# Fused attention and two feed-forward layers: score tiles kept in two standing PSUM buffers, written bank 1, 2, 0, and k/q transposes ahead of the fp32 ones

## The chip, the cores and the metric

The kernel runs on one core of a Trainium2 chip. A core has a matrix engine (TensorE, "PE" in the profile; its weight loads are "PEld"), a vector engine (DVE), a scalar engine (ACT), a general engine (GpSimd, "POOL"), a sync engine (SP) that issues DMAs, and 16 DMA engines. Each engine works through its own queue in the order of the program; engines wait for each other through semaphores. Matmul results go to PSUM, which is divided into banks of 512 fp32 columns. The metric is the device time of one execution in microseconds (us). Lower is better.

## The reference

```python
# q, k, v: (2, 8, 1152, 64) fp32
q_pool = q.reshape(B, H, S // 2, 2, D).mean(axis=3)          # 576 rows per head
scores = scale * np.matmul(q_pool, k.transpose(0, 1, 3, 2))  # 576 x 1152
scores = scores - np.max(scores, axis=-1, keepdims=True)
attn = np.exp(scores)
attn = attn / (np.sum(attn, axis=-1, keepdims=True) + 1e-09)
x = np.matmul(attn, v)                                       # then (1152, 512)
# then RMS norm, silu(x @ w_gate) * (x @ w_val) @ w_out,
# then h = x @ w_in;  out = (h * tanh(softplus(h))) @ w_out2
```

## The kernel before

fp32 operands are split into two fp16 halves, "hi" and "lo", and each product is made from three fp16 products (hi hi, hi lo, lo hi). The attention takes the first 275 us or so of the span, the two feed-forward layers the rest.

**Turns.** Attention is worked through two heads at a time. A pair of heads (`g` = 0 to 7, called pairs 1 to 8 below) has nine turns (`j` = 0 to 8), so there are 72 turns (`n` = 9 g + j). A turn is one block of 128 pooled query rows against all 1152 keys of a head; the turn for j = 8 holds the last 64 rows of each of the two heads. `attn_step(n)` (L700 to L722) writes a turn's instructions, and since the kernel runs under a manual schedule, the order of these calls is the order of each engine's queue:

- `scores(n)` (L237): PE writes a tile `s` of three PSUM banks, 384 columns used in each. Per bank there are two matmuls that add up in it (four of half width for j = 8). `ps_s` is a pool of two such tiles, taken in turn.
- `flip_pe(n-1)` (L297): three fp32 transposes on PE of a part of the turn before's exponentials `e`, into `ep`.
- `each(n, "pe")` calls `kq_flip` (L187): at j = 4 to 8, PE transposes up to eight fp16 blocks of the next pair's k and q (`khl`, `qhl`), into bank 0 of the tile `s` of turn n-1, whose scores have by then been read by the exponential.
- `split_hi`, `split_lo` and `flip` (n-1): ACT rounds a part of `e` to fp16 (`hl`, L282), POOL makes the lo half (L134), and SP issues a DMA transpose into `et`.
- `part_hi(n-1)` (L307): ACT rounds `ep` into `et` (L309).
- `each(n, "act")`: ACT casts of the next pair's k, q and v (L154, L178).
- `row_max(n)` (L259): DVE takes the maximum of the 1152 scores (L262) and scales it (L263).
- `each(n, "dve")` calls `kq_keep` (L201): at j = 4 to 8, DVE copies the transposed k and q out of bank 0 into `kqT` of the next pair (L203). This is the eviction of the title.
- `part_lo(n-1)` (L311): DVE makes the lo half of `ep` (L134 on DVE, `et<-ep,et`).
- `row_exp(n)` (L266): ACT's exponential of the whole tile `s` (L269).
- `attn_v(n-5)` (L319): 27 matmuls on PE (54 for j = 8) that weight v by `et` of five turns before, into `av`; then DVE's division (L356, L368, L370) where a block of x is done.
- `each(n, "scale")`: a DVE scaling of k, q or v (L141, L172) in some turns.

The tile `s` of turn n-1 is used again by `scores(n+1)`. The pool hands it over as a whole, so the first matmul of `scores(n+1)` stands behind the eviction that DVE makes in turn n. On DVE that eviction stands behind `row_max(n)`.

From n = 46 on, DVE, ACT and POOL also do RMS-norm steps (L461 to L490), and from n = 57 on the first steps of the weights' unpacking (`job_step`; L393 to L411), in between.

Of the kernel before, what the change touches and what calls it, by code (L numbers as in the profile page):

```python
# [9 lines left out]
F32 = mybir.dt.float32  # L10
F16 = mybir.dt.float16
# [29 lines left out]
def kernel(  # L41
# [13 lines left out]
    nc = tc.nc  # L55
# [16 lines left out]
    NTI = 2 * NI + 1  # L72
    NPR = B * NP
    NIT = B * NP * NTI
    SC = 3
# [5 lines left out]
    def pool(name, bufs, side="left", **kw):  # L81
        return tc.alloc_tile_pool(name=name, bufs=bufs, side=side, reuse_waits="tile", **kw)
# [28 lines left out]
    nat, kqT, vvt, cvt = {}, {}, {}, {}  # L111

    def load(w, g, i, eng=nc.scalar):

        if g >= NPR:
            return
        b, h0 = g // NP, 2 * (g % NP)
        if i == 0:
            nat[w, g] = nat_p.tile([128, 2, NJ, D] if w != "q" else [128, NTI, 2, D], F32, tag="nat", name=w + "n")
        t = nat[w, g]  # L120
        nm = NI * 128 * 2
        if w != "q":
            eng.dma_start(out=t[:, i], in_=(k if w == "k" else v)[b, h0 + i].rearrange("(p j) d -> p j d", j=NJ))
        elif i < 2:
            eng.dma_start(
                out=t[:, i * NI:(i + 1) * NI], in_=q[b, h0 + i, 0:nm, :].rearrange("(p i r) d -> p i r d", i=NI, r=2))
        else:
            for e in range(2):
                eng.dma_start(out=t[e * TL:(e + 1) * TL, 2 * NI],
                                  in_=q[b, h0 + e, nm:, :].rearrange("(p r) d -> p r d", r=2))  # L130
# [7 lines left out]
    def kv_scale(w, g):  # L138

        t = nat[w, g].rearrange("p h j (d z) -> p z (h j d)", z=2)  # L140
        nc.vector.tensor_scalar(out=t, in0=t, scalar1=QK_S if w == "k" else V_S, scalar2=None, op0=ALU.mult)  # L141

    def kv_hi(w, g, e):
        if e == 0:
            if w == "k":
                cvt["k", g] = cv_p.tile([128, 2 * NJ, 2 * D], F16, tag="khl", name="khl")
            else:
                t = kq_p.tile([128, 2 * NJ, 2 * D + 2], F16, tag="vv", name="vv")
                nc.gpsimd.memset(t[:, :, 2 * D:2 * D + 1], 1.0)
                vvt[g] = t  # L150
        t = (cvt["k", g] if w == "k" else vvt[g])[:, e * NJ:(e + 1) * NJ, :]
        o = 0 if w == "k" else D
        sc = 1.0 if g else QK_S if w == "k" else V_S
        nc.scalar.activation(out=t[:, :, o:o + D], in_=nat[w, g][:, e], func=ACTF.Copy, scale=sc)  # L154

    def kv_lo(w, g, e):
        t = (cvt["k", g] if w == "k" else vvt[g])[:, e * NJ:(e + 1) * NJ, :]
        o = 0 if w == "k" else D
        sc = 1.0 if g else QK_S if w == "k" else V_S
        lo_op(nc.gpsimd if g else nc.vector, t[:, :, D - o:2 * D - o], nat[w, g][:, e], sc, t[:, :, o:o + D])  # L160
        if e == 1:
            del nat[w, g]
# [11 lines left out]
    def q_hi(g):  # L174

        t = cv_p.tile([128, NTI, 3, D], F16, tag="qhl", name="qhl")
        a = cvt["s", g]
        nc.scalar.activation(out=t[:, :, 0:3:2, :], in_=a.unsqueeze(2).to_broadcast([128, NTI, 2, D]), func=ACTF.Copy)  # L178
        cvt["q", g] = t
# [18 lines left out]
            nc.tensor.transpose(out=ps[:, s - s0, :], in_=src, identity=ident)  # L198
        flips[g, s0] = (ps, n)

    def kq_keep(g, s0):  # L201
        ps, n = flips.pop((g, s0))
        nc.vector.tensor_copy(out=kqT[g][:, s0:s0 + n, :], in_=ps[:, 0:n, :])  # L203

    def kq_first():

        t = kqT[0] = kq_p.tile([128, 2 * NJ + 2 * NTI, 128], F16, tag="kqT", name="kqT")
        for s0, n in ((2 * NJ, 2 * NTI), (0, 2 * NJ)):
            e = 0 if s0 else 1
            kv_hi("v", 0, e)  # L210
            kv_lo("v", 0, e)
            ps = ps_s.tile([128, SC, 512], F32, tag="s", name="s").bitcast(F16)
            for s in range(s0, s0 + n):
                w, z = divmod(s - 2 * NJ, NTI)
                if s < 2 * NJ:
                    src = cvt["k", 0][:, s, :]
                else:
                    src = cvt["q", 0][:, z, w:w + 2, :].rearrange("p t d -> p (t d)")
                c, o = divmod(s - s0, 8)
                nc.tensor.transpose(out=ps[:, c, o * 128:(o + 1) * 128], in_=src, identity=ident)  # L220
            for c in range(-(-n // 8)):
                z = min(8, n - 8 * c)
                o = t[:, s0 + 8 * c:s0 + 8 * c + z, :]
                i = ps[:, c, 0:z * 128].rearrange("p (s t) -> p s t", s=z)
                if c == 1:
                    nc.vector.tensor_copy(out=o, in_=i)
                else:
                    nc.scalar.activation(out=o, in_=i, func=ACTF.Copy)

    def where(n):  # L230

        g, j = divmod(n, NTI)
        return g // NP, g, (j if g < NPR - 1 else (j - 1) % NTI)

    s_t, e_t, hl_t, et_t, av_t = {}, {}, {}, {}, {}

    def scores(n):  # L237
        b, g, j = where(n)
        kt = kqT[g][:, 0:2 * NJ, :]
        qt = kqT[g][:, 2 * NJ:, :]  # L240
        ps = ps_s.tile([128, SC, 512], F32, tag="s", name="s")
        heads = [(j % 2, j % 2 * NI + j // 2, 0, 128)] if j < 2 * NI else [
            (e, 2 * NI, e * TL, TL) for e in range(2)]
        per = SN // 128
        for c in range(SC):
            for e, slot, p0, m in heads:
                for w in range(2):
                    nc.tensor.matmul(  # L248
                        out=ps[p0:p0 + m, c, 0:SN],
                        lhsT=qt[:, w * NTI + slot, p0:p0 + m],  # L250
                        rhs=kt[:, e * NJ + c * per:e * NJ + (c + 1) * per, :].rearrange("p j t -> p (j t)"),
                        start=(w == 0),
                        stop=(w == 1),
                    )
        s_t[n] = ps

    mx, read = {}, {}
# [39 lines left out]
    def flip_pe(n):  # L297

        if n < 0:
            return  # L300
        e = e_t[n]
        ps = ps_t.tile([128, PB, 128], F32, tag="t", name="ep")
        for s in range(PB):
            nc.tensor.transpose(out=ps[:, s, :], in_=e[:, (NB + s) * 128:(NB + s + 1) * 128], identity=idf)  # L304
        ep_t[n] = ps
# [352 lines left out]
    def each(n, engine):  # L658

        g, j = n // NTI + 1, n % NTI  # L660
        if g >= NPR:
            return
        if engine == "load":
            if j in (0, 2):
                load("v", g, j // 2)
            elif j in (3, 4):
                load("k", g + 1, j - 3)
            elif j >= 6:
                load("q", g + 1, j - 6)
        elif engine == "act":  # L670
            if j in (2, 3):
                kv_hi("k", g, j - 2)
            elif j == 4:
                q_hi(g)
            elif j in (7, 8):
                kv_hi("v", g, j - 7)
        elif engine == "scale":
            if j in (1, 6):
                kv_scale("v" if j == 6 else "k", g)
            elif j == 2:  # L680
                q_scale(g)
        elif engine == "pool":
            if j in (2, 3):
                kv_lo("k", g, j - 2)
            elif j == 1:
                q_add(g)
            elif j == 4:
                q_lo(g)
            elif j in (7, 8):
                kv_lo("v", g, j - 7)  # L690
        elif j in FJ:
            f = FL[FJ.index(j)]
            if engine == "pe":
                kq_flip(read[n - 1], g, *f)
            else:
                kq_keep(g, f[0])

    FJ = (4, 5, 6, 7, 8)

    def attn_step(n):  # L700
        scores(n)
        flip_pe(n - 1)
        each(n, "pe")
        split_hi(n - 1)
        if n:
            split_lo(n - 1)
            flip(n - 1)
        part_hi(n - 1)
        x_sums()
        each(n, "act")  # L710
        row_max(n)
        each(n, "dve")
        part_lo(n - 1)
        row_exp(n)
        each(n, "pool")
        each(n, "load")
        if n >= LAG:
            attn_v(n - LAG)
            attn_r(n - LAG)
            attn_x(n - LAG)  # L720
        each(n, "scale")
        read.pop(n - 1, None)  # L722

    with tc.manual_schedule():
        nc.scalar.preload_act_table_set("natural_log_exp_and_others")
        ps_av = pool("ps_av", 1, space=PSUM)
        ps_t = pool("ps_t", 1, space=PSUM)
        ps_s = pool("ps_s", 2, space=PSUM)

        for w, i in (("q", 0), ("q", 1), ("q", 2), ("k", 0), ("k", 1), ("v", 0), ("v", 1)):  # L730
            load(w, 0, i, nc.sync)
# [61 lines left out]
        for step in TAIL:  # L793
# [5 lines left out]
            else:  # L799
                n = NIT - LAG + int(step)  # L800
# [114 lines left out]
```

## Time and profile before

| | us |
|---|---|
| median of 3 runs | 692.02 (690.71 to 693.10) |
| the profiled execution | 695.35 |
| its span, first to last instruction | 693.6 |
| attention, from the span's start | about 275 |

In the span's 693.6 us, PE is busy for 608.0 us, DVE for 462.5, ACT for 390.4 and POOL for 323.2. The span has two parts with different limits, and the page's row of slices shows them: in the slices of the attention DVE is at 8 and 9 tenths and PE at 7 or so, and after the attention PE is at 9 tenths. A row of a timeline gives the start (us from the span's start), the duration, the engine, the line, what is written and read, and in square brackets the time for which the engine had been idle and what ended that. Rows of matmuls are merged (x6 is six of them), and their ends are modelled.

### The profile page before, as it was taken

To read this page: it belongs to the slowest core of one execution; us is meant where nothing else is said; L and a number is where in the kernel's file an instruction comes from. 1 tells how busy PE (TensorE), PEld (TensorE's weight loads), DVE (VectorE), ACT (ScalarE), POOL (GpSimd) and SP (SyncE) were. 2 spreads that over 40 slices of the span, in tenths; PEclk is the share of its full clock that TensorE was granted. 3 is DMA by queue.
4 is the path that set the end of the run, shared out by engine and by line. 5 is a ranking of instruction groups with operands and counts; after the bars stand their busy time and mean duration, and the time that the engine had idled before them with its cause. 6 is when DMAs were issued, how large, how long until landed. Compare 5 with 4: busy or idle time off the path is not lost.

```text
span 693.6 us, 14705 instructions
## 1 busy us (share of the span) xinstructions
PE 608.0 (88%) x5880; PEld 428.1 (62%) x5880; DVE 462.5 (67%) x750; ACT 390.4 (56%) x654; POOL 323.2 (47%) x250
## 2 busy tenths in 40 slices
PE   3787778787676667799999999998999999999997
PEld 2466565666555556677777677776755555555553
DVE  4788888888899987559999962189289921111110
ACT  4888888898688586555555543144176623222221
POOL 0867878687689563057787772144033310000000
PEclk9799999999999899999999999999999999999999
DMA  6799899899899895344554430255245201000101
GB/s 185 135 191 185 175 179 171 185 186 176 150 172 222 171 186 104 71 122 124 156 175 156 153 122 1 61 167 168 62 126 176 95 0 46 1 1 15 31 1 45
DMA packets 161908, 84.05 MB, mean 121 GB/s; under 512 B 124720, under 2 KB 152368, under 8 KB 161840
## 3 DMA queue, kind: packets, MB, share of 16 engines
q1 hardware_dynamic: 151184, 67.71, 44.7%
q10 hardware_dynamic: 10656, 15.40, 8.4%
q8 instruction: 46, 0.75, 0.5%
q14 instruction: 22, 0.18, 0.1%
HBM read 50.07 MB, written 2.36 MB: 76 GB/s over the span
## 4 chain that ended last, share of the span: by engine, by line
PE 52%; DVE 32%; issue 7%; ACT 6%; DMA 2%; POOL 1%; SPq 0%; ACTq 0%; DVEq 0%
DVE m L262 9%; DVE c L402 6%; PE z L511 5%; PE z L513 4%; PE z L512 4%; PE po L648 4%; PE po L647 4%; PE po L646 4%; PE s L248 4%; ACT e L269 3%; PE py L511 3%; PE py L513 3%; PE py L512 3%; DVE c L400 3%; DVE c L404 2%
## 5 line engine op out<-in xcount | busy, mean ns | idle before, releaser
L134 POOL TENSOR_TENSOR hl<-e,hl 128x768 f16<-128x768 f32 x71 | 117.5, 1655 | 79.8 <-ACT hl L282 44.2
L248 PE MATMUL s<-kqT 128*128 128x384 f16 (+1 forms) x480 | 87.9, 342 | 28.3 <-DVE kqT L203 26.3
L269 ACT ACTIVATE e<-s,m 128x1152 f32<-128x1152 f32 x72 | 87.7, 1218 | 39.4 <-DVE m L263 35.2
L262 DVE TENSOR_REDUCE m<-s 128x1 f32<-128x1152 f32 x72 | 97.3, 1351 | 16.3 <-PE s L248 15.7
L136 DVE SCALAR_TENSOR_TENSOR g<-mo,g 128x384 f16<-128x384 f32 x48 | 26.9, 561 | 100.6 <-ACT g L621 100.6
L404 DVE SCALAR_TENSOR_TENSOR c<-raw,c 128x512 int32<-128x512 int32 x68 | 77.2, 1135 | 2.3
L134 POOL TENSOR_TENSOR stretch<-c,stretch 128x512 f16<-128x512 f32 x40 | 52.3, 1308 | 54.5 <-ACT stretch L411 54.4
L402 DVE SCALAR_TENSOR_TENSOR c<-gx,c 128x512 int32<-128x512 int32 x68 | 76.1, 1120 | 2.3
L333 PE MATMUL av<-vv,et 128*128 128x65 f16 (+1 forms) x720 | 76.4, 196 | 0.9 <-DVE x L370 0.9
L335 PE MATMUL av<-vv,et 128*128 128x64 f16 (+1 forms) x720 | 76.2, 195 | 0.0
L336 PE MATMUL av<-vv,et 128*128 128x65 f16 (+1 forms) x720 | 76.0, 197 | 0.0
L248 PEld LDWEIGHTS <-kqT 128*128 128x128 f16 (+1 forms) x480 | 43.1, 104 | 51.1 <-issue 33.8
L304 PE MATMUL ep<-idf,e 128*128 128x128 f32 x216 | 40.6, 300 | 36.3 <-ACT e L269 36.1
L333 PEld LDWEIGHTS <-et 128*128 128x128 f16 (+1 forms) x720 | 69.2, 103 | 2.2 <-issue 1.5
L335 PEld LDWEIGHTS <-et 128*128 128x128 f16 (+1 forms) x720 | 69.0, 102 | 0.5
L336 PEld LDWEIGHTS <-et 128*128 128x128 f16 (+1 forms) x720 | 69.0, 102 | 0.0
L134 POOL TENSOR_TENSOR h<-fo,h 128x288 f16<-128x288 f32 x48 | 48.8, 1017 | 37.5 <-ACT h L548 37.5
L615 ACT ACTIVATE mo<-z 128x384 f32<-128x384 f32 x48 | 23.2, 483 | 71.3 <-PE z L513 71.3
L282 ACT ACTIVATE hl<-e 128x768 f16<-128x768 f32 x72 | 60.7, 843 | 3.4 <-ACT e L269 1.5
L511 PE MATMUL z<-y,w2i 128*128 128x384 f16 x192 | 62.6, 326 | 0.0
L512 PE MATMUL z<-y,w2i 128*128 128x384 f16 x192 | 62.6, 326 | 0.0
L513 PE MATMUL z<-y,w2i 128*128 128x384 f16 x192 | 62.6, 326 | 0.0
(98 smaller groups left out, 1576.4 us busy)
## 6 DMA issues: line engine op xcount, KB each, us to landing
raw<-in_moe_w_out_dram SPq DMA_DIRECT2D x28, 512.0 KB, 3.4
raw<-in_moe_w_in_dram SPq DMA_DIRECT2D x16, 512.0 KB, 3.8
raw<-in_moe_w_gate_dram SPq DMA_DIRECT2D x8, 512.0 KB, 3.6
raw<-in_moe_w_val_dram SPq DMA_DIRECT2D x8, 512.0 KB, 3.5
vn<-in_v_dram ACTq DMA_DIRECT2D x14, 288.0 KB, 3.1
kn<-in_k_dram ACTq DMA_DIRECT2D x12, 288.0 KB, 4.4
qn<-in_q_dram ACTq DMA_DIRECT2D x12, 256.0 KB, 3.0
raw<-in_moe_w_gate_dram ACTq DMA_DIRECT2D x4, 512.0 KB, 4.9
```

The lines of the kernel that those rows point to most:

```text
L134: eng.tensor_tensor(out=out_, in0=in_, in1=hi, op=ALU.subtract)
L248: nc.tensor.matmul(out=ps[p0:p0 + m, c, 0:SN], lhsT=qt[:, w * NTI + slot, p0:p0 + m], rhs=kt[:, e * NJ + c * per:e * NJ + (c + 1) * per, : ...
L262: nc.vector.tensor_reduce(out=m[:, 0:1], in_=ps[:, :, 0:SN], op=ALU.max, axis=AXL.XY, negate=True)
L269: nc.scalar.activation(out=e.rearrange("p (c s) -> p c s", c=SC), in_=ps[:, :, 0:SN], func=ACTF.Exp, bias=m[:, 1:2], scale=s_scale)
L333: nc.tensor.matmul(out=av[0:m, o0:o0 + D + 1], lhsT=hi, rhs=vr[:, D:2 * D + 1], start=(jj == 0), stop=False)
L335: nc.tensor.matmul(out=av[0:m, o0:o0 + D], lhsT=hi, rhs=vr[:, 0:D], start=False, stop=False)
L336: nc.tensor.matmul(out=av[0:m, o0:o0 + D + 1], lhsT=et[:, z + (NB if jj < NB else PB), p0:p0 + m], rhs=vr[:, D:2 * D + 1], start=False, st ...
L402: nc.vector.scalar_tensor_tensor(out=c, in0=gi, scalar=-0x80000000, in1=c, op0=ALU.bitwise_and, op1=ALU.bitwise_or)
L404: nc.vector.scalar_tensor_tensor(out=c, in0=t[:, :, :, 0], scalar=29, in1=c, op0=ALU.logical_shift_right, op1=ALU.bitwise_or)
L511: nc.tensor.matmul(out=ps, lhsT=w0, rhs=x0, start=(i == 0), stop=False)
L512: nc.tensor.matmul(out=ps, lhsT=w0, rhs=x1, start=False, stop=False)
L513: nc.tensor.matmul(out=ps, lhsT=w1, rhs=x0, start=False, stop=(i == n - 1))
```

## The change

The two tiles `s` are taken from the pool once, as `s_buf`, and turn n uses `s_buf[n % 2]`, so that what a matmul waits for is tracked by what is read and written in the tile, and no longer by the handing over of the whole tile. `scores` writes bank 1 first, then bank 2, then bank 0. For banks 1 and 2 the dependence on the eviction, which reads bank 0 alone, is declared away; not so for j = 0, whose operands come from that pair's own `kqT`, filled by the evictions just before. And in `attn_step` the k/q transposes come ahead of the three fp32 transposes. The set-up for the first pair (`kq_first`) takes the same two buffers.

```diff
-    def kq_keep(g, s0):
+    def kq_keep(z, g, s0):
         ps, n = flips.pop((g, s0))
-        nc.vector.tensor_copy(out=kqT[g][:, s0:s0 + n, :], in_=ps[:, 0:n, :])
+        kept[z % 2] = nc.vector.tensor_copy(out=kqT[g][:, s0:s0 + n, :], in_=ps[:, 0:n, :])
...
-            ps = ps_s.tile([128, SC, 512], F32, tag="s", name="s").bitcast(F16)
+            ps = s_buf[e].bitcast(F16)
...
+    s_buf, kept = [], [None, None]
...
-        ps = ps_s.tile([128, SC, 512], F32, tag="s", name="s")
+        ps = s_buf[n % 2]
...
-        for c in range(SC):
+        for c in (1, 2, 0):
             for e, slot, p0, m in heads:
                 for w in range(2):
-                    nc.tensor.matmul(
+                    mm = nc.tensor.matmul(
...
+                    if c and n % NTI and kept[n % 2] is not None:
+
+                        tc.declare_no_dep(mm.ins, kept[n % 2].ins, reason="another bank")
+        kept[n % 2] = None
...
-                kq_keep(g, f[0])
+                kq_keep(n - 1, g, f[0])
...
         scores(n)
+        each(n, "pe")
         flip_pe(n - 1)
-        each(n, "pe")
...
+        s_buf += [ps_s.tile([128, SC, 512], F32, tag="s", name="s") for _ in range(2)]
```

On PE, at turn j = 6 of the first pair, these rows stood before: the scores (LDWEIGHTS and MATMUL in turn, six of each), the fp32 transposes `ep`, and the k/q transposes `khl` and `qhl`. "DVE_49" is DVE's semaphore, "Activation_49" ACT's, "Pool_49" POOL's; a row without brackets waits for no other engine.

```order
L248 LDWEIGHTS kqT
L248 MATMUL s<-kqT 128x384 [waits DVE_49]
L248 LDWEIGHTS kqT
L248 MATMUL s<-kqT 128x384
...
L304 MATMUL ep<-idf,e 128x128 [waits DVE_49,Activation_49]
L304 MATMUL ep<-idf,e 128x128 x2
L198 LDWEIGHTS khl
L198 MATMUL s<-ident,khl 128x128
...
L198 LDWEIGHTS qhl [waits Pool_49]
L198 MATMUL s<-ident,qhl 128x128
```

At the same place these stand now (the row that waits for DVE is the fifth of the six score matmuls):

```order
L249 LDWEIGHTS kqT
L249 MATMUL s<-kqT 128x384
...
L249 MATMUL s<-kqT 128x384 [waits DVE_49]
L249 LDWEIGHTS kqT
L249 MATMUL s<-kqT 128x384
L198 LDWEIGHTS khl
L198 MATMUL s<-ident,khl 128x128 [waits Activation_49]
...
L198 LDWEIGHTS qhl [waits Pool_49]
L198 MATMUL s<-ident,qhl 128x128
...
L309 MATMUL ep<-idf,e 128x128 [waits DVE_49]
L309 MATMUL ep<-idf,e 128x128 x2
```

The wait for DVE moved from the first matmul of the turn's scores to the fifth, the first of bank 0. The wait for ACT went with the k/q transposes, which now come first, and the fp32 transposes stand behind them and behind their wait for POOL.

On PE, at the next turn j = 8 and the turn j = 0 behind it, these rows stand now (half-width matmuls have 64 rows; before, the wait of the turn j = 8 stood on the first of its twelve):

```order
L249 LDWEIGHTS kqT
L249 MATMUL s<-kqT 64x384
...
L249 MATMUL s<-kqT 64x384 [waits DVE_49]
...
L198 MATMUL s<-ident,qhl 128x128 [waits Activation_49]
...
L309 MATMUL ep<-idf,e 128x128 [waits DVE_49]
L309 MATMUL ep<-idf,e 128x128 x2
...
L249 MATMUL s<-kqT 128x384 [waits DVE_49]
L249 LDWEIGHTS kqT
L249 MATMUL s<-kqT 128x384
```

Eight of the twelve matmuls of j = 8 moved ahead of the wait; at j = 0 the wait is still on the first matmul. The queues of DVE, ACT, POOL and SP hold the same instructions in the same order as before.

## Rows read from the trace of the kernel before

**Rows 1.** The page: DVE's busy tenths in 40 equal slices of the span.

```profile
DVE  4788888888899987559999962189289921111110
```

**Rows 2.** The waits, 14 to 275 us: engine and line, releaser: us, times, longest.

```profile
PE s L248 <- DVE kqT L203: 26.3, 27, 4.3
DVE m L262 <- PE s L248: 15.7, 26, 1.7
```

**Rows 3.** The timeline of DVE over the turns j = 5 to 8 of pair 4.

```profile
121.75 1.36 DVE L262 TENSOR_REDUCE m<-s 128x1 f32<-128x1152 f32 x1 [0.42 <-PE s L248]
...
123.22 0.69 DVE L203 COPY kqT<-s 128x1024 f16<-128x1024 f16 x1
123.83 0.55 DVE L134 TENSOR_TENSOR et<-ep,et 128x384 f16<-128x384 f32 x1
125.14 1.36 DVE L262 TENSOR_REDUCE m<-s 128x1 f32<-128x1152 f32 x1 [0.76 <-PE s L248]
...
128.95 1.35 DVE L262 TENSOR_REDUCE m<-s 128x1 f32<-128x1152 f32 x1
...
132.37 1.36 DVE L262 TENSOR_REDUCE m<-s 128x1 f32<-128x1152 f32 x1 [0.80 <-PE s L248]
...
135.49 1.36 DVE L262 TENSOR_REDUCE m<-s 128x1 f32<-128x1152 f32 x1 [0.17 <-PE s L248]
```

**Rows 4.** The timeline of PE there: scores of j = 5, 6, 8, and transposes.

```profile
120.56 1.15 PE L248 MATMUL s<-kqT 128*128 128x384 f16 x6
121.55 0.49 PE L304 MATMUL ep<-idf,e 128*128 128x128 f32 x3
121.88 0.61 PE L198 MATMUL s<-ident,khl 128*128 128x128 f16 x8
123.96 1.14 PE L248 MATMUL s<-kqT 128*128 128x384 f16 x6 [0.66 <-DVE kqT L203]
...
131.16 1.17 PE L248 MATMUL s<-kqT 128*64 128x384 f16 x12 [1.08 <-DVE kqT L203]
```

**Rows 5.** The score matmuls as one line: durations in ns, min/median/max.

```profile
L248 PE MATMUL s<-kqT x480: 322/326/528, 14.7 to 271.2; 128*128 128x384 f16 x128, 128*64 128x384 f16 x32
```

**Rows 6.** The timeline of PE and DVE in the first pair, turns j = 4, 5.

```profile
28.44 0.61 PE L198 MATMUL s<-ident,khl 128*128 128x128 f16 x8
...
29.16 0.69 DVE L203 COPY kqT<-s 128x1024 f16<-128x1024 f16 x1 [0.55 <-PE s L198]
...
29.90 2.08 PE L248 MATMUL s<-kqT 128*128 128x384 f16 x6 [0.85 <-DVE kqT L203]
...
32.02 1.36 DVE L262 TENSOR_REDUCE m<-s 128x1 f32<-128x1152 f32 x1 [1.71 <-PE s L248]
```

**Rows 7.** The timeline of ACT over the turns j = 6 to 8 of pair 4.

```profile
123.39 1.22 ACT L269 ACTIVATE e<-s,m 128x1152 f32<-128x1152 f32 x1 [0.82 <-DVE m L263]
124.64 0.84 ACT L282 ACTIVATE hl<-e 128x768 f16<-128x768 f32 x1
125.46 0.49 ACT L309 ACTIVATE et<-ep 128x384 f16<-128x384 f32 x1
...
133.23 0.68 ACT L154 ACTIVATE vv<-vn 128x576 f16<-128x576 f32 x1
134.01 1.23 ACT L269 ACTIVATE e<-s,m 128x1152 f32<-128x1152 f32 x1
```

**Rows 8.** The timeline of DVE and POOL in pair 6, turn j = 4.

```profile
183.03 0.15 DVE L469 TENSOR_TENSOR w<-w 128x5 f32<-128x5 f32 x1
183.21 1.56 DVE L470 TENSOR_TENSOR w<-w,w 128x5 f32<-128x5 f32 x1
183.11 1.64 POOL L134 TENSOR_TENSOR hl<-e,hl 128x768 f16<-128x768 f32 x1 [0.48 <-ACT hl L282]
```

**Rows 9.** Windows: busy us of each engine (instructions), clock, DMA share, GB/s.

```profile
104.00:164.00 60.00, 48.17 (x786) 37.78 (x786) 51.75 (x103) 53.85 (x75) 45.99 (x33) 1.00 0.95 183
...
200.00:240.00 40.00, 26.96 (x399) 20.85 (x399) 38.49 (x61) 29.36 (x41) 30.25 (x22) 0.91 1.07 201
```

## The prediction

> **What bounds the kernel now.** I first read the page's slices: in the attention DVE is at 8 and 9 tenths [rows 1], so what counts there is what DVE still waits for. The list of waits then names it: between 14 and 275 us DVE stands idle ahead of the row maximum 26 times, 15.7 us in all, for PE's scores, and PE in its turn stands idle ahead of the scores 27 times, 26.3 us in all, for the eviction of k and q [rows 2]. Only the 15.7 us can shorten the span, since PE's idle time ends in DVE's. The timelines of pair 4 show the loop [rows 3, 4]. In turn j = 5 the row maximum starts at 121.75, the eviction runs from 123.22 to 123.91, PE starts the next six score matmuls at 123.96, and the next row maximum starts at 125.14, after 0.76 us of idleness. The eviction stands behind the row maximum, the next scores behind the eviction, the next row maximum behind the scores: that ring of 3.39 us (125.14 less 121.75) is what sets the pace in these turns, and DVE's own work in it is 0.76 shorter.
>
> I then listed every row maximum of the timeline with its idle time. The waits for scores are of six sorts. 0.76 us at j = 6, in pairs 1 to 6 (six times). 0.79 or 0.80 at j = 8, in pairs 1 to 5 (five times). 1.71 once, at j = 5 of pair 1 [rows 6]. 0.42 at j = 5 of pairs 2 to 5, 0.17 to 0.20 at j = 0 of five pairs [rows 3], and five single ones that have no eviction ahead of them. At j = 7 DVE has a scaling of v to do and doesn't wait: 128.95 has no idle time [rows 3]. In pairs 6 and 7 DVE also has the RMS steps and the unpacking of weights, and all but the first j = 6 hides the ring.
>
> **The change, part by part.** *Bank order and the wait at the fifth matmul.* Six score matmuls take 1.14 us, one takes 0.326 [rows 4, 5], so one follows another after (1.14 - 0.326) / 5 = 0.163 us. Before, all six stand behind the eviction: the row maximum comes 125.14 - 123.91 = 1.23 us after its end. After, two do: 1.23 - 4 x 0.163 = 0.58. That puts the row maximum of j = 6 at 123.91 + 0.58 = 124.49. What is late next is DVE's own queue: its lo half of `ep` runs from 123.83 to 124.38 [rows 3]. So 0.65 of the 0.76 goes, and 0.11 stays. The four early matmuls need PE to be free for 4 x 0.163 = 0.65 us ahead of the eviction's end, and PE had been idle for 0.66 there [rows 4]: it just fits.
>
> At j = 8 the twelve half-width matmuls take 1.17 us [rows 4], so they follow each other after (1.17 - 0.33) / 11 = 0.076, and eight of them go ahead: 0.61 of the 0.80 goes. PE was idle for 1.08 there [rows 4], so it has the room.
>
> At j = 5 nothing goes: PE starts those scores at 120.56 without a wait [rows 4], behind the 54 matmuls of the half-width turn, so PE is the limit. At j = 0 the wait stays where it was. At j = 7 there was no idle time to take.
>
> Sum of the steady turns: 6 x 0.65 + 5 x 0.61 = 3.90 + 3.05 = 6.95 us.
>
> *The first pair, j = 5.* There are no weighted sums yet, so PE has nothing between the transposes and the scores. Before, the k/q transposes start at 28.44, the eviction at 29.16, with DVE idle for 0.55, and the six scores take 2.08 us from 29.90 to the row maximum at 32.02 [rows 6]. With the transposes first they start about 0.38 us sooner (three fp32 ones stand ahead of them now), so the eviction ends about 0.4 sooner, near 29.44; four of the six matmuls fit ahead of it or overlap it. At the slow spacing, (2.08 - 0.53) / 5 = 0.31 (0.53 is the longest single one [rows 5]), PE comes from the fp32 transposes near 29.0, needs 6 matmuls, about 2.1 us, and ends near 31.1: 0.85 gained. At the full clock's spacing the scores end before DVE's lo half of `ep` (0.6 us behind the eviction, near 30.1), which gives 1.9. I take 1.2, nearer the slow end, because slow is the level that this row shows.
>
> *The swapped transposes elsewhere.* The fp32 transposes now start later by the time of eight k/q ones, about 0.45 us (they take 0.61 with the last one's length [rows 4]). Behind them stand ACT's hi part of `ep` and, behind that, DVE's lo half. At j = 6 the k/q transposes wait for the exponential, which ends at 124.61 [rows 7]. Then 0.45 for them, 0.55 for the fp32 ones, 0.03 and 0.49 for ACT's part [rows 7] gives 126.15. DVE wants it 123.83 - 121.75 = 2.08 after its row maximum at 124.49, that is at 126.57: 0.4 to spare. At j = 8 the same working leaves 0.5. So the swap costs nothing in the steady turns, and its cover is DVE's row maximum and eviction, which stand ahead of the lo half. The fp32 transposes also come to stand behind the k/q ones' wait for POOL at j = 5 and 6; no row shows PE waiting for POOL there.
>
> *What is late next.* At j = 8 ACT casts v (0.68) between its hi part and the exponential [rows 7]. From one exponential to the next ACT then needs 1.25 (124.64 - 123.39) + 0.82 (125.46 - 124.64) + some 0.4 of the hi part + 0.7 for the cast, about 3.2 us, and DVE's new pace is 3.42 - 0.61 = 2.8. So that exponential is some 0.4 us late against DVE. It is wanted by the transposes and sums of the next turn on PE, and by the row maximum of the one after; following the rows of pair 3 to 5 forward, the row maximum at j = 1 comes about 0.3 late, but DVE's next instruction there waits for ACT's hi part anyway, and the delay is gone by j = 2.
>
> **The sum.** 6.95 + 1.2 = 8.15, say 8.1 us. Against the profiled execution, 695.35 us, that is 687.25; the median of the runs is 692.02 / 695.35 = 0.9952 of it, so 684.0 us.
>
> **The rivals.** *ACT takes the place of PE at j = 8.* If the 0.4 us above is not absorbed, and ACT's chain sets the turn, the five gains of 0.61 are lost: 684.0 + 3.0 = 687.0. For it: ACT's cast ends just as the exponential starts, at 134.01 with no idle time [rows 7]. Against it: the working above finds room two turns on.
>
> *DVE and POOL fall into other steps.* In pair 6 a product of 128 x 5 numbers takes DVE 1.56 us, where the one before it takes 0.15, and POOL had started an instruction 0.10 us before it; it ends with POOL's, at 184.75 [rows 8]. So where the two overlap, the later one pays, by up to 1.4 us. The change moves DVE against POOL by 0.1 to 0.65 us in pairs 6 and 7, where DVE has many such instructions. Three new stalls cost 3 x 1.4 = 4.2: 688.1. Two fewer give 2.4 to 2.8 (this one and the one behind it): 681.4. The Trainium skill, page "SBUF — State Buffer", section "Who interferes with whom", says the same as a rule: the two engines share a port pair, a DVE instruction with two SBUF inputs or in a two-port mode contends with GpSimd for it, and whoever issues first has it for its whole instruction while the other blocks. By that rule an instruction that moves by a tenth of a microsecond may win or lose a whole POOL instruction; the row agrees.
>
> *The DMA engines hold the pace.* Their share is 0.95 from 104 to 164 us [rows 9]. If that were full, pairs 2 to 5 would keep their time and 4 x 1.26 = 5.0 would be lost: 689.0. Against it: the share is 1.07 from 200 to 240 at 201 GB/s [rows 9], more than the 0.95 x 30.1 / 28.9 = 0.99 that is asked for.
>
> *Slower: the fp32 transposes come too late.* If they, and ACT's part behind them, arrive after DVE wants the lo half, DVE stands in the 28 turns that have eight k/q transposes. To be slower than 0.3% (2.1 us) it would have to lose 8.1 + 2.1 = 10.2 us, 0.36 per turn, so be late by 0.4 + 0.36 = 0.76 more than worked out. Matmuls at the slow spacing of pair 1 [rows 6] in every pair would do that, but the clock is 1.00 from 104 to 164 [rows 9]. It would give about 695.
>
> *The wait isn't gone.* If another dependence holds the first matmul, the time stays at 692.0. The order of PE's queue speaks against it: the first four matmuls carry no wait.
>
> **Chances.** The forecast 0.68, ACT 0.13, DVE and POOL (more stalls) 0.10, DMA 0.03, slower 0.04, no effect 0.02. Least gain within the forecast and its neighbours: the three new stalls, 688.1, with the first pair at 0.85 about 688.4. Most gain: the first pair at 1.9 (0.7 more) and two stalls fewer (2.4): 680.9. The range is 681.0 to 688.2, which leaves the DMA, the slower and the no-effect case out and cuts the ends. 0.3% (2.1 us) is about what a measurement of this kernel can tell from no change; below 689.9 lie the forecast, ACT, and most of the stalls and the DMA case: faster 0.91. Same: no effect and the rest of those, 0.05. Slower 0.04.
>
> **What the profile after would show.** Right: the waits of DVE for scores fall from 15.7 us to about 7 (0.11 at j = 6, 0.2 at j = 8, 0.42 and 0.17 as before), row maxima from j = 5 to 6 lie 2.74 us apart where it was 3.39, from j = 7 to 8 about 2.8 where it was 3.42, and pair 4 takes 28.9 us where it took 30.1 (135.49 less the same turn of the pair before, 105.38). ACT rival: the spacing from j = 8 to j = 2 grows by what j = 8 gained. Stalls: an RMS or unpacking row of DVE lengthens by a microsecond or more in pairs 6 and 7. Slower: DVE is idle ahead of its lo half of `ep`, waiting for ACT. Wrong altogether: PE still idle for the eviction with no score matmul in front of it.

## The result, and the profile after

The changed kernel takes 685.12 us (median; 683.04 to 688.62), the kernel before 692.11 us beside it (690.71 to 693.10). The ratio is 0.990, with a 95% interval of 0.9854 to 0.9947: 1.0% faster, or 7.0 us. The profiled execution took 687.06 us with a span of 685.3 us, 8.3 us less than the span before.

From the first row maximum to the last the attention took 256.02 us before (15.98 to 272.00) and takes 247.72 (17.18 to 264.90): 8.30 us less, where the prediction's sum was 8.15. The first row maximum itself came 1.2 us later, and the work behind the last one took 1.2 us less (693.56 - 272.00 = 421.56 before, 685.27 - 264.90 = 420.38 after), so that the two cancel. Neither is an effect of the change: in the other ten executions that were traced, of whichever order, the first row maximum came at 15.53 to 17.29, and what stands behind the last took 420.13 to 421.52. Nor is 8.30 the gain of every execution: second executions of both kernels took 254.46 and 249.81 for the same stretch, 4.65 less.

The page's slices show DVE fuller: of the first fourteen, six stand at 9 tenths, where three did [rows 1].

```profile
DVE  3889988989898996569999943289299921110110
```

The waits from 14 to 275 us, in the same columns as [rows 2] (engine and line, releaser: us, times, longest). Most line numbers are five higher after the change: the row maximum is L267, the exponential L274; the scores are L249, and the eviction is still L203.

```profile
PE s L249 <- DVE kqT L203: 14.9, 17, 2.7
...
DVE m L267 <- PE s L249: 10.4, 21, 2.3
```

PE's wait for the eviction fell from 26.3 to 14.9 us, and DVE's wait for scores from 15.7 to 10.4.

The timeline of DVE over the turns j = 5 to 8 of pair 4 and the j = 0 and 1 behind them, which answers [rows 3]:

```profile
118.61 1.36 DVE L267 TENSOR_REDUCE m<-s 128x1 f32<-128x1152 f32 x1 [0.42 <-PE s L249]
...
120.08 0.69 DVE L203 COPY kqT<-s 128x1024 f16<-128x1024 f16 x1
120.69 0.55 DVE L134 TENSOR_TENSOR et<-ep,et 128x384 f16<-128x384 f32 x1
121.35 1.36 DVE L267 TENSOR_REDUCE m<-s 128x1 f32<-128x1152 f32 x1
...
125.16 1.35 DVE L267 TENSOR_REDUCE m<-s 128x1 f32<-128x1152 f32 x1
...
127.92 1.36 DVE L267 TENSOR_REDUCE m<-s 128x1 f32<-128x1152 f32 x1
...
131.04 1.36 DVE L267 TENSOR_REDUCE m<-s 128x1 f32<-128x1152 f32 x1 [0.17 <-PE s L249]
...
133.44 1.36 DVE L267 TENSOR_REDUCE m<-s 128x1 f32<-128x1152 f32 x1 [0.37 <-PE s L249]
```

From j = 5 to 6 the row maxima lie 121.35 - 118.61 = 2.74 us apart (3.39 before), from j = 7 to 8 they lie 127.92 - 125.16 = 2.76 apart (3.42 before). Of the idle times, 0.76 and 0.80, only 0.11 (121.35 - 121.24, the end of the lo half of `ep`) and 0.14 are left, too short for a bracket in the row.

The scores on PE at j = 6 and j = 8 there, which answer [rows 4]:

```profile
120.01 1.30 PE L249 MATMUL s<-kqT 128*128 128x384 f16 x6
...
125.95 0.84 PE L249 MATMUL s<-kqT 128*64 128x384 f16 x8
127.37 0.52 PE L249 MATMUL s<-kqT 128*64 128x384 f16 x4 [0.57 <-DVE kqT L203]
```

At j = 8 the split is plain to see: eight matmuls run from 125.95 on, ahead of the eviction's end (126.62 + 0.69 = 127.31), and four at 127.37 behind it. PE still waits for the eviction, but with four matmuls left to do instead of twelve. At j = 6 the six start at 120.01, 0.07 us before the eviction does.

To compare kernels place by place I measure a pair by the distance from its first row maximum to the next pair's (pair 8: to the last). In us, one profiled execution each; "again" is a second execution of the same kernel:

| pair | before | before again | after | after again |
|---|---|---|---|---|
| 1 | 29.79 | 28.95 | 28.22 | 28.23 |
| 2 | 29.80 | 29.80 | 28.44 | 28.44 |
| 3 | 29.81 | 29.79 | 28.44 | 28.44 |
| 4 | 30.11 | 30.11 | 28.76 | 28.75 |
| 5 | 29.81 | 29.80 | 28.97 | 28.96 |
| 6 | 35.01 | 35.20 | 34.25 | 35.37 |
| 7 | 40.17 | 39.91 | 38.93 | 39.56 |
| 8 | 31.52 | 30.90 | 31.71 | 32.05 |

Pairs 2 to 5 repeat within 0.02 us, so differences of a tenth can be read there. Pairs 6 to 8 differ by up to 1.1 us between two executions of one kernel, and pair 1 by 0.8, so there they can't.

### The profile page after: what moved, and what is told of

Its sections match the earlier page's. It is cut to its first block, busy times and chain, and to the rows that moved or that the text cites. A ratio compares the mean times of both kernels' runs of the same rounds, so it can differ in the third digit from the quotient of the medians.

```text
span 685.3 us, 14671 instructions
## 1 busy us (share of the span) xinstructions
PE 608.5 (89%) x5880; PEld 424.5 (62%) x5880; DVE 460.4 (67%) x750; ACT 390.7 (57%) x654; POOL 324.5 (47%) x250
## 4 chain that ended last, share of the span: by engine, by line
PE 44%; DVE 12%; issue 5%; ACT 2%; POOL 0%; DMA 0%; ACTq 0%; DVEq 0%
DVE c L407 5%; PE z L516 5%; PE z L518 5%; PE z L517 5%; PE po L652 4%; PE po L653 4%; PE po L651 4%; PE py L516 3%; PE py L518 3%; PE py L517 3%; DVE c L405 2%; DVE fo L546 2%; DVE c L409 2%; PE pv L518 1%; PE pv L516 1%
## 5 line engine op out<-in xcount | busy, mean ns | idle before, releaser
L274 ACT ACTIVATE e<-s,m 128x1152 f32<-128x1152 f32 x72 | 87.8, 1219 | 30.7 <-DVE m L268 26.9
L267 DVE TENSOR_REDUCE m<-s 128x1 f32<-128x1152 f32 x72 | 97.3, 1351 | 11.6 <-PE s L249 10.4
L249 PE MATMUL s<-kqT 128*128 128x384 f16 (+1 forms) x480 | 90.0, 341 | 16.8 <-DVE kqT L203 14.9
L249 PEld LDWEIGHTS <-kqT 128*128 128x128 f16 (+1 forms) x480 | 40.7, 103 | 41.8 <-issue 25.1
```

What stands on the lines that cost most here:

```text
L249: mm = nc.tensor.matmul(out=ps[p0:p0 + m, c, 0:SN], lhsT=qt[:, w * NTI + slot, p0:p0 + m], rhs=kt[:, e * NJ + c * per:e * NJ + (c + 1) * p ...
L267: nc.vector.tensor_reduce(out=m[:, 0:1], in_=ps[:, :, 0:SN], op=ALU.max, axis=AXL.XY, negate=True)
L274: nc.scalar.activation(out=e.rearrange("p (c s) -> p c s", c=SC), in_=ps[:, :, 0:SN], func=ACTF.Exp, bias=m[:, 1:2], scale=s_scale)
```

## The experiments

Four questions were open: which part of the change brings the gain, whether the price of a matmul moved ahead of the wait is as worked out, what makes pairs 6 and 7 vary, and whether a version is faster than both kernels. All diffs are against the changed kernel. One execution of each was traced, so that a reading of its rows holds for that execution. The times:

| kernel | median, us | ratio to before, 95% interval |
|---|---|---|
| the change | 685.12 | 0.990 (0.9854 to 0.9947) |
| e1, transposes in the old order | 684.14 | 0.9864 (0.9823 to 0.9904) |
| e2, wait on the first matmul | 691.65 | 0.9975 (0.9953 to 0.9998) |
| e3, one bank ahead of the wait | 685.82 | 0.9885 (0.9862 to 0.9908) |
| e4, RMS products a turn later | 684.74 | 0.9875 (0.9850 to 0.9900) |
| e7, e4 and sums of squares later | 684.01 | 0.9868 (0.9835 to 0.9901) |
| e8, e7 with transposes in the old order | 685.45 | 0.9875 (0.9831 to 0.9920) |
| e9, RMS steps from n = 41 | 690.92 | 0.9969 (0.9948 to 0.9989) |
| e10, RMS steps from n = 50 | 683.81 | 0.9873 (0.9846 to 0.9901) |

**e1: the banks without the swap.** My theory was that the place of the wait brings the gain of the steady turns and the swap part of the first pair's; the rival, that the swap brings some of it everywhere.

```diff
         scores(n)
-        each(n, "pe")
         flip_pe(n - 1)
+        each(n, "pe")
```

> The changed kernel with the fp32 transposes ahead of the k/q ones again; banks in the order 1, 2, 0 with the wait at bank 0 as in the change. Theory (the gain comes from the four score matmuls ahead of the wait; the swap only pays in pair 1 and costs something where ACT is full, in pair 5): row maxima from j = 5 to 6 stay 2.74 us apart in pairs 2 to 4 and from j = 7 to 8 at 2.77, pair 5 gets back its 0.5 us (2.74 where the change has 3.17), pair 1 loses about 1 us; in all 685 to 686.5 us. Rival (it is the earlier k/q transposes that shorten the ring): the spacings go back to 3.4 us and the time to about 691.

The row maxima of j = 5, 6, 7 and 8 of a steady pair:

```profile
90.16 1.36 DVE L267 TENSOR_REDUCE m<-s 128x1 f32<-128x1152 f32 x1 [0.42 <-PE s L249]
...
92.90 1.36 DVE L267 TENSOR_REDUCE m<-s 128x1 f32<-128x1152 f32 x1
...
96.70 1.35 DVE L267 TENSOR_REDUCE m<-s 128x1 f32<-128x1152 f32 x1
...
99.47 1.36 DVE L267 TENSOR_REDUCE m<-s 128x1 f32<-128x1152 f32 x1
```

92.90 - 90.16 = 2.74 and 99.47 - 96.70 = 2.77: all of the gain without the swap. Pairs 3 and 4 take 28.50 and 28.79, 0.03 to 0.06 more than with it, and j = 4 to 5 takes 4.31 where the change has 4.26 (before had 4.31). So the swap is worth 0.05 us a pair there. (Pair 2 took 28.80, 0.31 of that between j = 0 and 2; in e8, also without the swap, it takes 28.50.) In pair 1 the two spacings around the first eviction (j = 4 to 6) add up to 7.24 without the swap and 7.45 with it. The rival fell, and with it my reading that the swap brings the first pair's gain. Pair 5 got back little more than half of what I expected: 2.91 from j = 5 to 6, not 2.74.

**e2: the swap and the banks' order, but the wait on the first matmul.**

```diff
-                    if c and n % NTI and kept[n % 2] is not None:
...
-                        tc.declare_no_dep(mm.ins, kept[n % 2].ins, reason="another bank")
```

> The changed kernel without the declared independence: two standing buffers, banks 1, 2, 0, transposes swapped, but the first score matmul waits for the eviction again. Theory (the wait's place is the whole gain of the steady turns): spacings 3.39 from j = 5 to 6 and 3.42 from j = 7 to 8 as before, only pair 1 keeps up to 0.9 us; 690.5 to 692 us. Rival (the standing buffers or the swap carry part of it): 686 to 689 us, with spacings well under 3.3.

```profile
92.36 1.36 DVE L264 TENSOR_REDUCE m<-s 128x1 f32<-128x1152 f32 x1 [0.42 <-PE s L249]
...
95.75 1.36 DVE L264 TENSOR_REDUCE m<-s 128x1 f32<-128x1152 f32 x1 [0.76 <-PE s L249]
...
102.97 1.36 DVE L264 TENSOR_REDUCE m<-s 128x1 f32<-128x1152 f32 x1 [0.80 <-PE s L249]
```

The idle times 0.76 and 0.80 are back to the hundredth, j = 5 to 6 takes 3.39 again, and pairs 2 and 3 take 29.74, within 0.07 us of before. In these turns two standing buffers and a new order of banks bring nothing by themselves beyond the 0.05 at j = 4 to 5 that goes with the swap; the gain is the wait that moved to the fifth matmul. The total agrees: its ratio, 0.9975, is 0.2% off 1, where the change has 1.0%. The Trainium skill, page "PSUM — Partial Sum Buffer", section "PSUM bank collisions raise a hardware error", asks for semaphores that guard PSUM by bank. This run guards the whole tile and the changed kernel the one bank that is read: 3.39 against 2.74 us at j = 6.

**e3: one bank ahead of the wait instead of two.**

```diff
-        for c in (1, 2, 0):
+        for c in (1, 0, 2):
```

> The changed kernel with banks in the order 1, 0, 2: two score matmuls (four at j = 8) ahead of the wait in place of four (eight). Theory (each matmul ahead of the wait is worth its own spacing, 0.163 us, at j = 8 0.076): 0.33 of 0.65 at j = 6 and 0.30 of 0.61 at j = 8 are kept, spacings 3.06 and 3.1; 11 places lose 0.32 each, 3.5 us, 688.6 us. Rival (any matmul ahead of the wait is enough, since what counts is that PE is awake): spacings 2.74 and 2.77, 685 us.

```profile
89.78 1.36 DVE L267 TENSOR_REDUCE m<-s 128x1 f32<-128x1152 f32 x1 [0.42 <-PE s L249]
...
92.84 1.36 DVE L267 TENSOR_REDUCE m<-s 128x1 f32<-128x1152 f32 x1 [0.44 <-PE s L249]
...
96.64 1.35 DVE L267 TENSOR_REDUCE m<-s 128x1 f32<-128x1152 f32 x1
...
99.73 1.36 DVE L267 TENSOR_REDUCE m<-s 128x1 f32<-128x1152 f32 x1 [0.47 <-PE s L249]
```

92.84 - 89.78 = 3.06 and 99.73 - 96.64 = 3.09, which is half of the way, as worked out: a score matmul taken from behind the wait brings 0.163 us each, (3.39 - 3.06) / 2 = 0.165. The total missed: 685.8, not the 688.6 expected, and by their totals e3 and the change can't be told apart (their intervals overlap). In the steady pairs this kernel lost what it should (pair 3: 29.08 against 28.44), but in the traced execution pair 6 came 2.5 us shorter than in the changed kernel's first execution. That is followed up next.

**What pairs 6 and 7 do (the traces above, and e5 and e6).** e5 and e6 are second executions of the changed kernel and of the kernel before.

> The changed kernel once more, another execution. Theory (what is left between executions is whether TensorE falls to 1.2 GHz over the 54 matmuls of turn j = 4 in pairs 6 and 7, and what DVE then collides with on POOL): pairs 2 to 5 repeat to 0.1 us (28.44, 28.44, 28.76, 28.97), while j = 4 of pair 6 is 4.95 or 7.8 us and j = 4 and 5 of pair 7 together 10.3, 11.5 or 12.9. Rival (these places are fixed by the kernel's code): all places repeat, 7.78 and 10.33.

> The kernel before once more. Theory: pairs 2 to 5 repeat to 0.1 us (29.80, 29.81, 29.81 to 30.11, 29.81), and j = 4 of pair 6 and j = 4, 5 of pair 7 may be other than 7.89 and 11.51 us. Rival: they repeat as they are.

They took 687.58 and 691.97 us, and pairs 2 to 5 repeated, as the table shows. The places that I had expected to vary came close to repeating as well: j = 4 to 5 of pair 6 took 8.31 (7.78 in the first execution) and 8.09 (7.89), j = 4 to 6 of pair 7 took 10.34 (10.34) and 11.53 (11.51). So here the rival was nearer. Across kernels the spacing from j = 4 to 5 of pair 6 has two levels, and they go with the clock that was granted while PE did the 54 half-width weighted sums there (a stretch of 3.2 us, cut at the same distance behind the row maximum of j = 4 in each; the runs that move the products of that turn, e4 and e7 to e10, are left out):

| execution | granted clock there | j = 4 to 5, us |
|---|---|---|
| before, before again | 0.54, 0.51 | 7.89, 8.09 |
| after, after again | 0.54, 0.60 | 7.78, 8.31 |
| e1, e2, e3 | 1.00, 1.00, 1.00 | 4.95, 4.95, 4.96 |

The windows of the kernel after, a stretch ahead of those sums and the sums (us, PE busy and count, clock, DMA share, GB/s):

```profile
170.00:174.00 4.00, 2.00 (x29) 1.00 0.73 123
174.40:177.60 3.20, 3.20 (x56) 0.54 1.04 266
```

The same in e3:

```profile
171.45:175.45 4.00, 2.00 (x29) 1.00 0.76 131
175.85:179.05 3.20, 3.20 (x70) 1.00 0.99 257
```

Ahead of the sums PE was busy for 2.00 of 4.00 us in both; then one execution was granted 0.54, about the lower of the two levels (1.2 GHz of 2.4), and the other 1.00. No kernel was traced at both levels at this place, so whether the level there goes with the kernel or with the execution is not shown. How a microsecond of slow matmuls becomes three shows on DVE. The kernel after, from the division of the sums to the next row maximum:

```profile
177.10 0.15 DVE L361 TENSOR_SCALAR r<-av 64x2 f32<-64x2 f32 x1 [1.54 <-PE av L341]
...
178.07 1.51 DVE L476 TENSOR_SCALAR w<-w 128x5 f32<-128x5 f32 x1
179.61 1.19 DVE L477 TENSOR_TENSOR w<-w,w 128x5 f32<-128x5 f32 x1
180.72 1.34 DVE L267 TENSOR_REDUCE m<-s 128x1 f32<-128x1152 f32 x1
```

POOL in that stretch:

```profile
177.90 1.65 POOL L134 TENSOR_TENSOR hl<-e,hl 128x768 f16<-128x768 f32 x1 [0.56 <-ACT hl L287]
179.51 1.27 POOL L483 TENSOR_TENSOR xn<-x,gbc 128x512 f32<-128x512 f32 x1
```

The same instructions on DVE in e3:

```profile
177.57 0.15 DVE L361 TENSOR_SCALAR r<-av 64x2 f32<-64x2 f32 x1 [0.57 <-PE av L341]
...
179.06 0.17 DVE L476 TENSOR_SCALAR w<-w 128x5 f32<-128x5 f32 x1
179.27 0.17 DVE L477 TENSOR_TENSOR w<-w,w 128x5 f32<-128x5 f32 x1
```

Where the sums end late (1.54 us of idleness instead of 0.57), the products of 128 x 5 numbers meet POOL: L476 starts 0.17 us behind POOL's subtraction and ends with it (178.07 + 1.51 = 179.58; 177.90 + 1.65 = 179.55), and L477 ends at 180.80 with POOL's next instruction (179.51 + 1.27 = 180.78). In e3 POOL's subtraction started at 179.35, when the products were all but done, and these took 0.17 each. So the sums end 1.0 us later, and the two meetings add 1.34 + 1.02; e3 lost 0.5 at L474 ahead of these rows (0.67 for 0.15), which leaves the 2.8 us between 7.78 and 4.96. This is the pattern of [rows 8]. The Trainium skill, page "SBUF — State Buffer", section "Who interferes with whom", says that DVE and GpSimd share a port pair and the later one blocks for the whole instruction; these ends agree within 0.03 us.

**e4: the products a turn later.** If the meeting with POOL is the price, moving the four products out of it should take it away even at the low clock.

```diff
-        steps = [[s0], [s1], [s2]] + [[] for _ in range((z1 - z0 - 1) * every + 4)]
+        steps = ([[s0], [s1], [], [s2]] if b == 0 else [[s0], [s1], [s2], []]) + [[] for _ in range((z1 - z0 - 1) * every + 3)]
```

> The changed kernel with the four small RMS products of the first batch (128 x 5, on DVE) one turn later, ahead of POOL's multiplication rather than beside POOL's subtraction in pair 6, turn j = 4. Theory (two of them stand 1.3 and 1.0 us behind POOL instructions there): the row maxima from j = 4 to 5 of pair 6 come 5.6 us apart where the change has 7.78, PE's scores set them; the products take 0.2 us each a turn later and cost DVE 0.7 there; 1.4 to 2 us gained, about 683.5 us. Rival (the four products are long wherever they stand, or another wait takes the place): no gain, 685 us.

```profile
177.67 1.36 DVE L267 TENSOR_REDUCE m<-s 128x1 f32<-128x1152 f32 x1 [0.89 <-PE s L249]
...
180.40 0.17 DVE L475 TENSOR_TENSOR w<-w,w 128x5 f32<-128x5 f32 x1
```

It did: the clock was 0.53 at those sums, yet j = 4 to 5 took 5.73 instead of 7.78, and the turn behind it, now with the four products, 3.22 instead of 2.73. That is 2.05 less 0.49, 1.6 us gained in an execution at the low clock. DVE now waits 0.89 for scores, since PE is still slow. It is no cure at the full clock: in e8 below, which has the same products a turn later and no swap, the clock at those sums was 1.00 and j = 4 to 5 took 4.32, but then the products came early enough to meet POOL in the next turn (two of them took 0.92 and 1.63), which took 5.45.

**e7 and e8: the best of these, with and without the swap.** Pair 5 loses 0.43 us against pairs 2 to 4, at j = 5 to 6 (below). I moved ACT's sums of squares (L458) behind the exponential.

```diff
         part_hi(n - 1)
-        x_sums()
...
         row_exp(n)
+        x_sums()
```

(on top of e4; e8 also puts the transposes back as in e1.)

> The changed kernel with the four RMS products one turn later, and ACT's sums of squares behind the exponential rather than ahead of it. Theory: pair 5 takes 28.4 to 28.5 us (0.55 us of waiting at j = 5 gone, since ACT's exponential no longer stands behind the sum of squares); pair 6, j = 4 is 5.0 to 5.7 us whatever the clock; pair 7 still varies; 682.5 to 684 us, with less spread than the change. Rival (the sums of squares don't hold the exponential, or hold the next turn's instead): pair 5 stays at 28.97.

> As e7_best_swap, but with the fp32 transposes ahead of the k/q ones as in the kernel before. Theory (the swap is worth nothing): within 0.3 us per pair of e7_best_swap in pairs 1 to 5, pair 5 at 28.4 to 28.7, and 682.5 to 684.5 us. Rival (the swap is worth something once ACT is relieved): every pair 0.2 us or more longer, 1 to 2 us in all.

A miss. At j = 5 to 6 of pair 5 the spacing fell to 2.74 as wanted, but pair 5 took 29.14, more than the 28.97 of the change: 0.42 came back at j = 0 and 0.22 at j = 4, because a sum of squares behind one exponential holds up the next turn's rounding on ACT, and then the fp32 transposes and the exponential after it. The row maximum of j = 1 of pair 5 in e7 shows it:

```profile
130.05 1.36 DVE L267 TENSOR_REDUCE m<-s 128x1 f32<-128x1152 f32 x1
...
132.85 1.36 DVE L267 TENSOR_REDUCE m<-s 128x1 f32<-128x1152 f32 x1 [0.59 <-PE s L249]
```

e7 and e8 agree within 0.07 us in each of pairs 2 to 5, so the swap brings no more here than in e1. (e8's other differences lie in pairs 1 and 6 to 8, where the granted clock differs: 0.65 from j = 3 to 6 of pair 1, where e7 has 1.00.)

**e9 and e10: the RMS steps five turns earlier, or four later.**

```diff
-RMS0 = 46
+RMS0 = 41
```

> The changed kernel with the RMS steps of the first batch five turns sooner (RMS0 = 41 for 46): the first step and the four small products come to pair 5, j = 6 and j = 8, where POOL has gaps, in place of pair 6, j = 2 and j = 4, where POOL is full. Theory (the 2.8 to 3.3 us that vary at j = 4 of pair 6 come from DVE running into POOL's instructions there, after a stretch that left PE cold): pair 6, j = 2 falls from 4.35 to 3.2 and j = 4 from 7.8 to 4.3; up to 1 us is given back at pair 5, j = 8, where POOL casts v, and the xh products collide in other turns; 681 to 683.5 us. Rival (the work costs the same wherever it stands): pairs 5 to 7 together as in the change, 685 us.

e9 missed by 7 us. The steps met POOL earlier (pair 5 took 31.71, with products of 1.09 and 1.50), and one turn of pair 7 took 10.66 us (pair 7 as a whole 40.11, 1.2 more than in the change): an instruction of ACT stood behind a DMA that had not landed, and DVE behind ACT. ACT there:

```profile
205.14 0.72 ACT L488 ACTIVATE xh<-xn,w 64x512 f16<-64x512 f32 x1 [4.48 <-DMA stretch<-xh]
```

The other direction, `RMS0 = 50`:

> The changed kernel with the RMS steps of the first batch four turns later (RMS0 = 50 for 46): first step and products at pair 6, j = 6 and j = 8, xh products in pairs 7 and 8, beside the unpacking of weights. Theory: pair 6, j = 2 and j = 4 fall to 3.2 and 4.3 as in e9_rms_41, but more xh products stand in pairs 7 and 8, where DVE is full already and their time adds up there; 683 to 686 us. Rival (the same wherever it stands): 685 us, with 7.8 us at some other turn.

Pair 6's j = 2 and j = 4 came as expected: 3.18 and 4.26. But the products were not gone; they met POOL again at j = 8:

```profile
188.81 1.16 DVE L475 TENSOR_TENSOR w<-w,w 128x5 f32<-128x5 f32 x1
...
190.20 1.50 DVE L477 TENSOR_TENSOR w<-w,w 128x5 f32<-128x5 f32 x1
```

Its 683.81 us (683.55 to 684.32) is the lowest median and the narrowest spread of all, but its interval overlaps the change's: it may be a microsecond better, and that isn't shown.

Not tried: letting the first four matmuls of j = 0 go ahead as well. Their operands, the pair's own `kqT`, come out of the evictions just before, so there they really depend on them.

## Why the prediction was right, and where it wasn't

684.0 was forecast and 685.12 measured; the profiled gain was 8.30 us against 8.15. That agreement is better than its parts, and in part luck: the second executions of both kernels differ by 4.65 us over the same stretch, and the medians by 7.0.

**Right: the mechanism and its price.** At j = 6, 0.65 of the 0.76 was to go: the spacing fell from 3.39 to 2.74 in pairs 2, 3, 4 and 6, and the 0.11 that was to stay stayed. At j = 8, 0.61 was worked out and 0.65 came (3.41 to 2.76): the row maximum came 1.26 us behind the eviction's end before, not the 1.23 of j = 6, and 0.61 now. e2 shows that the wait's place is the cause, e3 that it is paid per matmul. Pairs 2 to 5 gained 119.53 - 114.61 = 4.92 us, where 4 x 1.26 = 5.04 was worked out. j = 7 and the start of j = 5 stayed, as said.

**Right: the delay at j = 1.** It was forecast at 0.3, gone by j = 2. j = 0 to 1 takes 2.38 instead of 2.17, and j = 1 to 2 takes 3.67 instead of 3.88: 0.21 late, and 0.21 given back. So the rival that ACT takes PE's place at j = 8 fell.

**Half right: the swap costs nothing.** In the steady turns it costs nothing, and brings 0.05 a pair at j = 4 to 5. In pair 5 the step failed: j = 5 to 6 took 3.17, not 2.74, in both executions (3.39 before). There ACT has a sum of squares to do ahead of a cast, so the exponential comes late:

```profile
144.63 0.62 ACT L458 ACTIVATE sq<-x 128x512 f32<-128x512 f32 x1
...
146.29 1.21 ACT L274 ACTIVATE e<-s,m 128x1152 f32<-128x1152 f32 x1
```

PE's transposes wait for it, and the next scores stand behind them and the weighted sums:

```profile
147.56 0.61 PE L198 MATMUL s<-ident,khl 128*128 128x128 f16 x8 [0.45 <-ACT e L274]
148.00 0.50 PE L309 MATMUL ep<-idf,e 128*128 128x128 f32 x3
...
149.15 1.14 PE L249 MATMUL s<-kqT 128*128 128x384 f16 x6
```

The eviction had started at 148.62 in that turn, so the scores began only 0.16 us ahead of its end (149.31), and DVE stood for 0.55 at the row maximum. I had taken pair 4 for all steady pairs and not looked at ACT in pair 5; without the swap (e1) the loss is 0.17 there instead of 0.43. So the swap costs 0.26 there. A wait of PE for POOL, which I had ruled out at j = 5 and 6, came at j = 4 of pair 6 (2.00 us ahead of the k/q transposes); DVE evicted them there without idle time. The other place where the traces show the swap costing something is the first pair (below).

**Wrong: the first pair's term.** I gave its j = 5 1.2 us, and with its j = 6 1.85. The spacings of j = 3 to 6 there add up to 10.26 before, 9.42 before again, 9.35 after: a gain of 0.07 to 0.91. Two things were wrong.

The first is the base. The 2.08 us for six matmuls [rows 6] belonged to that execution, not to the kernel: the granted clock was 0.54 from 29.50 to 33.00 us. In the second execution of before it was 1.00 there, the same six took 1.14 us, and the idle time of the row maximum behind them was 0.76 instead of 1.71 (the slow ones were the scores of j = 4, 2.13 us at a granted clock of 0.50):

```profile
29.57 1.14 PE L248 MATMUL s<-kqT 128*128 128x384 f16 x6 [0.85 <-DVE kqT L203]
```

So I had counted slow matmuls of one execution as a cost of the order of work.

The second is ACT at j = 6. The j = 5 gained about what I gave it, or more: from the row maximum of j = 3 to that of j = 5 it takes 6.85 before and 6.03 before again, and 4.87 after. But from j = 5 to 6 it takes 4.48, where 3.41 and 3.39 stood before: not 0.65 less, but 1.07 more. In that turn ACT has a cast of q to do ahead of the exponential:

```profile
30.63 1.16 ACT L178 ACTIVATE qhl<-qs 128x1152 f16<-128x1152 f32 x1
31.68 1.21 ACT L274 ACTIVATE e<-s,m 128x1152 f32<-128x1152 f32 x1
```

PE's k/q transposes wait for the exponential, and DVE's eviction for them:

```profile
32.95 0.61 PE L198 MATMUL s<-ident,khl 128*128 128x128 f16 x8 [1.75 <-ACT e L274]
33.66 0.69 DVE L203 COPY kqT<-s 128x1024 f16<-128x1024 f16 x1 [0.88 <-PE s L198]
```

So once PE's wait is gone, ACT sets this turn. I had asked what is late next at j = 8 alone. And the swap doesn't help there: e1 without it has 9.15 for the same three spacings, 0.20 less, since the hi part of `ep` waits for transposes that come later and the exponential behind it starts 5.32 us behind the row maximum of j = 3 with the swap and 5.05 without. The term was too big by 0.9 to 1.8 us.

**Not forecast: pairs 6 to 8.** Beyond the j = 6 of pair 6 they gave 0.11 + 1.24 - 0.19 = 1.16 us in the profiled executions, which made up for the first pair. That is luck. It is all in pair 7, where j = 4 to 6 takes 11.51 and 11.53 before and 10.34 and 10.34 after, and what differs there is the granted clock at the sums of j = 4: 1.00 before, in both executions, and 0.61 and 0.55 after. At the lower clock DVE stands 1.4 us longer for the sums, and two unpacking steps behind them then all but miss POOL's instructions: they take 0.57 and 0.69 us, where before they took 1.81 and 2.01 (POOL had started an instruction 0.12 us ahead of the first and 0.22 us ahead of the second). The second of them, before and after:

```profile
224.34 2.01 DVE L404 SCALAR_TENSOR_TENSOR c<-raw,c 128x512 int32<-128x512 int32 x1
```

```profile
218.17 0.69 DVE L409 SCALAR_TENSOR_TENSOR c<-raw,c 128x512 int32<-128x512 int32 x1
```

e8, with the changed banks and a clock of 1.00 there, takes 11.52 as before did; e1 and e2, at 0.57 and 0.50, meet POOL with another instruction and take 12.85 and 12.86.

**The sum again, by the steady places alone:** 4 x 0.65 + 0.22 at j = 6, 5 x 0.65 at j = 8, 0.05 x 4 at j = 5, that is 2.82 + 3.25 + 0.20 = 6.3 (ten turns, and the 0.05 of pairs 2 to 5), and 0.1 to 0.9 in the first pair: 6.4 to 7.2, where the medians differ by 7.0.

**DVE's waits fell to 10.4 us, not to 7.** What I hadn't counted: 0.35 at j = 1 in five pairs (1.8), 0.55 in pair 5, 0.71 at j = 6 of pair 1, 1.1 more at the first two row maxima of all, and at j = 6 of pair 8 2.31 where before had 1.74 (other executions of either order have 0.59). On the other side, the 0.11 and 0.14 that are left at j = 6 and 8, which I had counted, are too short for the list. (The prediction counts the waits at j = 0 as five and the single ones as five; they are six and four, which changes no sum.)

**The other rivals.** The DMA rival fell: its share is 1.00 from 104 to 164 us, where pairs 4 and 5 got shorter, and 1.10 from 44 to 104. Compare [rows 9]:

```profile
44.00:104.00 60.00, 51.67 (x826) 39.02 (x826) 54.52 (x108) 53.63 (x68) 48.85 (x35) 1.00 1.10 198
104.00:164.00 60.00, 50.42 (x816) 38.28 (x815) 53.46 (x104) 55.98 (x77) 47.05 (x34) 1.00 1.00 182
```

The slower rival fell as well: DVE doesn't wait for its lo half of `ep` at j = 5 to 8 of pair 4 (120.69 above has no idle time), and from 14 to 275 us its waits for ACT ahead of the lo half fell, from 4.6 to 3.2 us. The rival of DVE and POOL was right in kind and in place, but at j = 4 of pair 6 it strikes before and after alike, and in pair 7 the meetings came and went with the granted clock.

## What to carry to other kernels

When a buffer of several banks is written again, write the bank whose reader is latest at the end, and see that the wait stands on that bank's first matmul alone; each matmul that moves ahead of the wait is worth its spacing (0.163 us here), until the next engine's own queue is full, or a third engine in the ring is late, as ACT was in the first pair. A span that contains places which differ by 1 to 3 us for other reasons than the edit can't judge an edit of 1 us: compare the spacings of one recurring instruction at places that repeat, and read a wait that is to go in more than one execution and in every repetition of the loop.

## What the runs showed of the hardware

I had not expected the granted clock to differ at the same place between executions of one kernel: in the first pair of the kernel before it was 0.54 from 29.50 to 33.00 us in one execution and 1.00 in the other, and six score matmuls took 2.08 and 1.14 us. At j = 4 of pair 6 it was 0.51 to 0.60 in two executions each of before and after and 1.00 in one each of e1, e2 and e3, with PE busy 2.00 of 4.00 us ahead of the sums in all seven. The 54 matmuls lose 1.0 us by it, and two products of 128 x 5 numbers, 0.17 us each on their own, lose 1.34 and 1.02 more because they then meet POOL. In pair 7 the lower clock was the faster one, 10.34 us against 11.51, because there DVE missed POOL by coming later. What decides the clock the traces don't show.
